# A retention layer with routed experts: where the rows of x are transposed, and by which engine they are copied

## The chip, the cores and the metric

One core of one Trainium2 chip runs the whole program as a single launch. The metric is the device time of that launch in microseconds, the median of several runs. The engines are named as in the profile: PE (TensorE's matmuls) and PEld (its weight loads), DVE (VectorE), ACT (ScalarE), POOL (GpSimd), SP (SyncE, which here only issues transfers).

## The reference

Eight batches of eight heads, 576 positions, 64 values per head. The first part is attention without softmax: scores are multiplied by a decay that falls with distance, and what lies in the future is zero. Its output, one row of 512 values for each of 4,608 tokens, goes through a layer of eight experts, of which each token takes the one with the largest logit.

```python
scores = scale * np.matmul(q, k.transpose(0, 1, 3, 2))
gamma = 1.0 - 2.0 ** (-5.0 - np.arange(H, dtype=np.float32))
rel = pos[:, None] - pos[None, :]
Dmat = np.where(rel >= 0, gamma[:, None, None] ** rel[None, :, :], 0.0)
ret = scores * Dmat[None, :, :, :]
x = np.matmul(ret, v)                      # then (B, S, H, D) -> (B * S, H * D)
...
logits = x @ w_gate
expert_idx = np.argmax(logits, axis=1)
probs = np.exp(logits - logits.max(-1, keepdims=True))
probs /= probs.sum(-1, keepdims=True) + 1e-09
gate_w = probs[np.arange(N), expert_idx]
for e in range(E):
    mask = expert_idx == e
    h = np.maximum(x[mask] @ w1[e], 0.0)
    out[mask] = gate_w[mask, None] * (h @ w2[e])
```

## The kernel before

The order of the work is written out by hand: each engine executes its instructions in the order in which the program issues them, and the framework adds the semaphores. For PSUM the framework orders accesses of different engines by whole banks of a tile.

**The attention stage** is one loop over 40 blocks (L792), five for each batch: c = 0 to 3 are chunks of 128 positions, c = 4 is the remainder of 64. The decay is put into q and k beforehand (scale_q, scale_k, on GpSimd), so that a chunk needs the product of its own scores, masked to the causal half, with v, and the product of its q with a running state. One turn i of the loop works on several blocks at once, in this order on TensorE:

- stage_T transposes k of block i + 2 and, but for c = 0, a quarter of the next batch's q, eight transposes each, into the tile pst2 (L325, L327). ScalarE copies kT (L316) and qT (L302) out.
- stage_R transposes block i - 2 of the finished xT (features by tokens) back into rows of tokens: eight f32 transposes of 64 by 64, in c = 4 four, into the upper 64 of each 128 columns of the score tile pssc, which the scores overwrite later (L459). ScalarE copies one half of the columns and VectorE the other, both to bf16 in the tile xr (L462), and SP writes the rows to x_rows in HBM (L467, L470).
- steps (L812) lets some of the small VectorE instructions of the routing go.
- stage_S adds block i + 1 to the running state in pss (L345), and stage_se copies the state to SBUF on ScalarE (L356). The tile se has two buffers.
- stage_AV multiplies the masked scores of block i with v into psx (L404).
- product (in c = 2 and 3) is a routing product; in c = 0 and 1 stage_L1 and stage_L2 compute the gate's logits of the batch before. All use the PSUM tile of stage_T.
- stage_SC computes the scores of block i + 1 into pssc, two banks, one for each of the two heads of a pair (L374, L387); VectorE multiplies them with the mask into sc (L377, one instruction for each bank) or, for the remainder, with tri (L389, one for both).
- stage_IN adds q times the state to psx (L417; in c = 4 both products of the remainder, L433 and L439), and ScalarE copies the result to xT (L421), in c = 4 to xo, to which VectorE adds the other half (xTr, L444).

Loads of q, k, v go by SP's queue, each held back by a mark (the copy or mask of an earlier block); load_k and load_v run six blocks ahead. The experts' weights and the gathers go by GpSimd's queue, some of them within the loop.

**Routing.** route_batch is a generator of some 25 VectorE instructions for each batch, two products on TensorE among them; a step hands back what it costs, and steps lets go so many as the budget of the turn allows.

**The expert stage** follows from L828 on: gathered rows are transposed, multiplied with w1 and w2 in bf16, scaled by the gate, and scattered to the output. The last two stage_R run there, in the PSUM pool psT.

Of the kernel before, what the change touches and what calls it, by code (L numbers as in the profile page):

```python
# [43 lines left out]
def kernel(  # L44
# [22 lines left out]
    def after(ins, dep):  # L67

        if dep is not None:
# [21 lines left out]
    wk3 = p1.enter_context(tc.tile_pool(name="wk3", bufs=3))  # L91
    wk4 = p1.enter_context(tc.tile_pool(name="wk4", bufs=4))
# [9 lines left out]
             "R": lambda n: [pssc[:, o, :].rearrange("p (a u t) -> p a u t", u=2, t=DH)[:, 0:n, 1, :]  # L102
                             for o in range(2)]}
# [84 lines left out]
    nc.gpsimd.tensor_copy(out=identb[:, :], in_=ident[:, :])  # L188
    nc.vector.tensor_scalar(out=tok[:, 0, :], in0=tok[:, 0, :], scalar1=-1.0, scalar2=None, op0=ALU.mult)
# [30 lines left out]
    pssc = ps1.tile([P, 2, 512], F32, name="pssc")  # L220
# [47 lines left out]
    mark = {}  # L268
# [81 lines left out]
    def stage_se():  # L350

        if not todo_s:
            return
        b, c = blocks[todo_s.pop()]
        se = wkp.tile([P, NP, DH], F32, tag="se")
        mark["se"] = nc.scalar.copy(out=se[:, :, :].rearrange("p a d -> p (a d)"), in_=pss[:, 0:NP * DH])  # L356
        sts[(b, c + 1)] = se
# [3 lines left out]
    def stage_SC(i):  # L361
# [6 lines left out]
        if c < NCH:  # L368
            qT = qTs[b]
            for p in range(NP):  # L370
                for u in range(2):
                    for j in range(2):
                        r = slice(j * DH, (j + 1) * DH)
                        mm(pssc[u * DH:(u + 1) * DH, j, p * P + u * DH:(p + 1) * P], kT[r, p, u * DH:(u + 1) * DH],  # L374
                           qT[r, p, c * P + u * DH:(c + 1) * P], True, True)
            for j in range(2):
                mark["sc"] = nc.vector.tensor_tensor(  # L377
                    out=sc[:, j, :, :], in0=pssc[:, j, :].rearrange("p (a i) -> p a i", i=P),
                    in1=mask[:, :].unsqueeze(1).to_broadcast([P, NP, P]), op=ALU.mult)
        else:  # L380
            qTs[(b, "r")] = kT
            for p2 in range(2):
                for hf in range(2):
                    p = 2 * hf + p2
                    for j in range(2):
                        r = slice(j * DH, (j + 1) * DH)
                        mm(pssc[hf * DH:(hf + 1) * DH, j, p2 * P + DH:(p2 + 1) * P], kT[r, p, DH:P], kT[r, p, 0:DH],  # L387
                           True, True)
            mark["sc"] = nc.vector.tensor_tensor(  # L389
                out=sc[:, :, 0:2, 0:DH],  # L390
                in0=pssc[:, :, :].rearrange("p j (a u i) -> p j a u i", u=2, i=DH)[:, :, 0:2, 1, :],
                in1=tri[:, :].unsqueeze(1).unsqueeze(1).to_broadcast([P, 2, 2, DH]), op=ALU.mult)
# [54 lines left out]
    def stage_R(i):  # L447

        b, c = blocks[i]
# [3 lines left out]
        src = xTs[b][:, c, :] if full else xTs[(b, "r")][:, :]  # L453


        for k in range(n):
            for o in range(2):
                r = slice(o * DH, (o + 1) * DH)
                tr(ps[o][:, k ^ 2 * o if full else k, :], src[r, k * P:(k + 1) * P], ident[r, r])  # L459
        xr = wk4.tile([P, n * P], BF16, tag="xr", name="xr")  # L460
        t0 = b * S + c * P
        for o, copy in enumerate((nc.scalar.copy, nc.vector.tensor_copy)):  # L462
            hs = (slice(0, 4, 3), slice(1, 3))[o]
# [557 lines left out]
```

## Time and profile before

| | |
|---|---|
| median of 3 runs | 372.52 us (371.15 to 372.71) |
| the profiled execution | 369.17 us, its span 367.5 us |
| mean granted TensorE clock | 0.962 of full speed |
| busy in the span: PE, PEld | 321.4 us (87%), 236.4 us (64%) |
| DVE, ACT, POOL | 148.4 us (40%), 156.6 us (43%), 199.5 us (54%) |

The span goes from the first to the last instruction of one profiled execution, which is 1.7 us shorter than that execution's own time. Matmuls are pipelined and their ends are modelled, so a busy PE is not at its peak; the starts of weight loads (PEld) tell best when TensorE got to a piece of work. The attention stage ends at about 202 us.

### The profile page before, as it was taken

What the parts mean: (1) busy time and instruction counts of PE and PEld (TensorE: products, weight loads), DVE (VectorE), ACT (ScalarE), POOL (GpSimd) and SP (SyncE); (2) the same over time, 40 slices, a digit from 0 to 9 for tenths busy, and PEclk for the clock granted to TensorE, in tenths of its full rate; (3) what the DMA queues carried; (4) which work ended last, traced back from release to release, by engine and by line L of the source; (5) the groups of instructions that cost most, each with busy time, mean ns of one, the idle gap of its engine ahead of it and who ended that gap; (6) DMA issues with size and microseconds to landing.
All of it is one profiled execution on the core that took longest, in us unless ns stands there. A gap on an engine that the chain in (4) does not pass through costs nothing. (4 is left out here: it accounts for less than half of the span.)

```text
span 367.5 us, 12120 instructions
## 1 busy us (share of the span) xinstructions
PE 321.4 (87%) x5108; PEld 236.4 (64%) x5108; DVE 148.4 (40%) x442; ACT 156.6 (43%) x331; POOL 199.5 (54%) x255
## 2 busy tenths in 40 slices
PE   5898988979888889787876997999999999999991
PEld 5687867767677677676765765555565656565650
DVE  5234446465564565654735363221121212121211
ACT  3345344352443434444313433345545454545440
POOL 2467534625355236468730026577778778788422
PEclk9599999999999999999996799899999999999997
DMA  8999978979696978999999013379899999999312
GB/s 209 222 221 213 241 188 206 215 194 208 147 230 163 210 181 187 210 224 218 195 192 167 23 58 96 117 134 190 186 212 208 222 193 206 214 192 214 138 58 75
DMA packets 117577, 65.95 MB, mean 179 GB/s; under 512 B 88334, under 2 KB 109838, under 8 KB 117520
## 3 DMA queue, kind: packets, MB, share of 16 engines
q0 software_dynamic: 18432, 31.80, 41.5%
q1 hardware_dynamic: 98560, 33.34, 39.0%
q8 instruction: 41, 0.67, 0.8%
q14 instruction: 16, 0.13, 0.1%
q10 hardware_dynamic: 528, 0.02, 0.1%
HBM read 67.45 MB, written 15.50 MB: 226 GB/s over the span
## 5 line engine op out<-in xcount | busy, mean ns | idle before, releaser
L283 POOL TENSOR_TENSOR kk<-kt,kg 128x512 f32<-128x512 f32 x39 | 40.8, 1045 | 85.9 <-PE pss L62 50.1
L62 PE MATMUL py<-w2b,ht 128*128 128x512 bf16 x320 | 76.0, 384 | 0.3 <-DVE ys L884 0.3
L739 ACT ACTIVATE ht<-pm 128x384 bf16<-128x384 f32 (+1 forms) x96 | 50.6, 527 | 57.3 <-PE pm L62 56.6
L62 PE MATMUL pm<-xt,w1b 128*128 128x256 bf16 (+1 forms) x512 | 73.2, 301 | 0.0
L884 DVE TENSOR_SCALAR ys<-py,gsl 128x512 f32<-128x512 f32 x40 | 30.0, 751 | 105.2 <-PE py L62 100.0
L885 POOL DMA_INDIRECT out_dram<-ys,tids x40 | 40.8, 1019 | 58.0 <-ACT xt L724 24.1
L62 PEld LDWEIGHTS <-w1b 128*128 128x128 bf16 x512 | 50.1, 99 | 22.0 <-issue 0.2
L377 DVE TENSOR_TENSOR sc<-pssc,mask 128x512 f32<-128x512 f32 x64 | 41.3, 686 | 29.5 <-PE pssc L62 24.2
L62 PEld LDWEIGHTS <-ht 128*128 128x128 bf16 x320 | 30.3, 99 | 31.3 <-issue 1.8
L679 POOL DMA_INDIRECT xg<-x_rows,tidg x40 | 41.1, 1026 | 11.8 <-issue 8.4
L62 PE MATMUL pssc<-qT,kT 64*64 64x64 f32 (+1 forms) x1024 | 35.8, 259 | 4.5 <-DVE xr L464 4.5
L62 PE MATMUL psx<-sc,vt 128*64 128x128 f32 (+1 forms) x640 | 39.6, 269 | 0.1
L356 ACT COPY se<-pss 128x256 f32<-128x256 f32 x32 | 12.2, 380 | 49.8 <-PE psx L62 44.2
L724 ACT COPY xt<-pt 128x512 bf16<-128x512 bf16 x40 | 22.8, 586 | 23.2 <-PE pt L65 23.2
L62 PEld LDWEIGHTS psx<-sc,vt 128*64 128x64 f32 (+1 forms) x640 | 32.1, 140 | 0.8 <-ACT xT L421 0.3
L62 PEld LDWEIGHTS pssc<-qT,kT 64*64 64x64 f32 x1024 | 27.9, 135 | 7.3 <-DVE xr L464 5.4
L421 ACT COPY xT<-psx 128x512 f32<-128x512 f32 x32 | 18.8, 586 | 30.1 <-PE psx L62 19.3
L464 DVE CAST xr<-pssc 128x256 bf16<-128x256 f32 (+1 forms) x38 | 15.2, 400 | 37.2 <-ACT xr L464 37.2
L273 POOL TENSOR_TENSOR qq<-qt,qg 128x512 f32<-128x512 f32 x28 | 29.8, 1064 | 0.1
L316 ACT COPY kT<-pst 128x512 f32<-128x512 f32 x40 | 23.7, 592 | 13.5 <-PE pst L65 12.7
L261 POOL DMA_DIRECT2D w2b<-in_moe_w_dram x32 | 23.5, 755 | 4.5 <-DMA w2b<-in_moe_w_dram 2.2
L62 PE MATMUL pss<-vt,kk 128*64 128x64 f32 x512 | 23.3, 234 | 0.5 <-issue 0.5
(130 smaller groups left out, 366.0 us busy)
## 6 DMA issues: line engine op xcount, KB each, us to landing
kt<-in_k_dram SPq DMA_DIRECT2D x32, 256.0 KB, 4.8
qt<-in_q_dram SPq DMA_DIRECT2D x16, 512.0 KB, 5.8
vt<-in_v_dram SPq DMA_DIRECT2D x32, 256.0 KB, 4.4
w1b<-in_moe_w_dram POOLq DMA_DIRECT2D x32, 256.0 KB, 6.5
w2b<-in_moe_w_dram POOLq DMA_DIRECT2D x32, 256.0 KB, 5.6
x_rows<-xr SPq DMA_DIRECT2D x32, 128.0 KB, 5.0
kt<-in_q_dram SPq DMA_DIRECT2D x8, 128.0 KB, 4.7
kt<-in_k_dram SPq DMA_DIRECT2D x8, 128.0 KB, 5.3
```

Source lines behind the costliest of these rows:

```text
L62: nc.tensor.matmul(out=out, lhsT=lhsT, rhs=rhs, start=start, stop=stop, skip_group_check=True)
L261: after(nc.gpsimd.dma_start(out=wb[e][part // n][:, o:o + m, :], in_=w[e, o * P:(o + m) * P, :].rearrange("(c p) f -> p c f", p=P)), dep)
L273: eng.tensor_tensor(out=qq[:, :, :].rearrange("p s (h d) -> p h s d", d=DH), in0=qts[b][:, h0:h0 + 2, :, :], in1=qg[:, 0:NCH, h0:h0 + 2].r ...
L283: eng.tensor_tensor(out=kk[:, :, :], in0=kts.pop(i)[:, :, :], in1=kg[:, blocks[i][1], :].unsqueeze(2).to_broadcast([P, H, DH]), op=ALU.mult)
L316: mark["kT"] = nc.scalar.copy(out=kT[:, :, :].rearrange("p a (u t) -> p u a t", u=2), in_=ps[:, :, o:o + 256].rearrange("p u (a t) -> p u ...
L377: mark["sc"] = nc.vector.tensor_tensor(out=sc[:, j, :, :], in0=pssc[:, j, :].rearrange("p (a i) -> p a i", i=P), in1=mask[:, :].unsqueeze( ...
L421: mark["xT"] = nc.scalar.copy(out=xTs[b][:, c, :].rearrange("p (w t) -> p w t", w=2), in_=psx[:, :, 0:2 * P])
L679: nc.gpsimd.indirect_dma_start(out=xg[:, :], out_offset=None, in_=x_rows[0:nr, :], in_offset=bass.IndirectOffsetOnAxis(ap=slots[ph][1][:, ...
L724: nc.scalar.copy(out=xts[(e, ph)][:, :, j * P:(j + 1) * P], in_=pt[:, :, :])
L739: nc.scalar.activation(out=ht[:, f0:f0 + per, :], in_=pm[:, :, :], func=AF.Relu)
L884: nc.vector.tensor_scalar(out=ys[:, :], in0=py[:, :], scalar1=gsl[:, e, slots[ph][2] + j:slots[ph][2] + j + 1], scalar2=None, op0=ALU.mult)
L885: scatters.append(nc.gpsimd.indirect_dma_start(out=next(outs)[:, :], out_offset=bass.IndirectOffsetOnAxis(ap=slots[ph][0][:, e, j:j + 1], ...
```

## The change

- stage_S now stands in front of stage_R (in c = 4 behind it), and both in front of steps; get_TQ, the copy of qT, stands in front of both.
- The score tile of two banks becomes two tiles of one bank each. Each mask instruction reads one tile; the remainder's mask becomes two instructions.
- stage_xb, new: ScalarE casts block i - 1 of xT from f32 to a bf16 tile xb in SBUF. stage_R transposes that one turn later: eight bf16 transposes (four in c = 4) with 64 weight columns and 128 moving columns, into the first score tile alone, read as bf16. A second identity with its halves swapped (identx) puts the heads in their right order. One ScalarE copy of all columns writes xr; VectorE's copy is gone.
- se has three buffers instead of two.
- In c = 4 stage_IN stands in front of stage_SC.

```diff
--- before.py
+++ after.py
@@ -89,6 +89,7 @@
     ldv = p1.enter_context(tc.tile_pool(name="ldv", bufs=6))
     wkp = p1.enter_context(tc.tile_pool(name="wk", bufs=2))
     wk3 = p1.enter_context(tc.tile_pool(name="wk3", bufs=3))
+    wkb = p1.enter_context(tc.tile_pool(name="wkb", bufs=3))
     wk4 = p1.enter_context(tc.tile_pool(name="wk4", bufs=4))
     wk1 = p1.enter_context(tc.tile_pool(name="wk1", bufs=1))
     attc = p1.enter_context(tc.tile_pool(name="attc", bufs=1))
@@ -99,8 +100,7 @@
     ps1 = pp.enter_context(tc.tile_pool(name="ps1", bufs=1, space=PSUM))
     pst2 = pp.enter_context(tc.tile_pool(name="pst2", bufs=1, space=PSUM))
     pools = {"S": lambda *a: pst2.tile(*a, tag="t2", name="pss2"),
-             "R": lambda n: [pssc[:, o, :].rearrange("p (a u t) -> p a u t", u=2, t=DH)[:, 0:n, 1, :]
-                             for o in range(2)]}
+             "R": lambda n: pssc[0][:, :].bitcast(BF16).rearrange("p (a u t) -> p a u t", u=2, t=P)[:, 0:n, 1, :]}

     blocks = [(b, c) for b in range(B) for c in range(NCOL)]
@@ -186,6 +186,9 @@
     make_identity(nc, ident[:, :])
     identb = consts.tile([P, P], BF16, name="identb")
     nc.gpsimd.tensor_copy(out=identb[:, :], in_=ident[:, :])
+    identx = consts.tile([P, P], BF16, name="identx")
+    for j in range(2):
+        nc.gpsimd.tensor_copy(out=identx[:, j * DH:(j + 1) * DH], in_=ident[:, (1 - j) * DH:(2 - j) * DH])
     nc.vector.tensor_scalar(out=tok[:, 0, :], in0=tok[:, 0, :], scalar1=-1.0, scalar2=None, op0=ALU.mult)
     lrow = attc.tile([P, 2, H], F32, name="lrow")
     for h in range(H):
@@ -217,7 +220,7 @@

-    pssc = ps1.tile([P, 2, 512], F32, name="pssc")
+    pssc = [ps1.tile([P, 512], F32, name=f"pssc{j}") for j in range(2)]
     psx = ps1.tile([P, 2, 512], F32, name="psx")
     pss = ps1.tile([P, 512], F32, name="pss")

@@ -265,7 +268,17 @@

     qqs, qTs, kks, kTs, scs, sts, xTs, lts = {}, {}, {}, {}, {}, {}, {}, {}
-    mark = {}
+    xbs, mark = {}, {}
+
+    def stage_xb(i):
+
+        if i < 0:
+            return
+        b, c = blocks[i]
+        src = xTs[b][:, c, :] if c < NCH else xTs[(b, "r")][:, :]
+        xbs[i] = wkb.tile([P, src.shape[-1]], BF16, tag="xb", name="xb")
+        nc.scalar.copy(out=xbs[i][:, :], in_=src)
+

     def scale_q(b, p, eng=nc.gpsimd):
         h0 = 2 * p
@@ -352,7 +365,7 @@
         if not todo_s:
             return
         b, c = blocks[todo_s.pop()]
-        se = wkp.tile([P, NP, DH], F32, tag="se")
+        se = wk3.tile([P, NP, DH], F32, tag="se")
         mark["se"] = nc.scalar.copy(out=se[:, :, :].rearrange("p a d -> p (a d)"), in_=pss[:, 0:NP * DH])
         sts[(b, c + 1)] = se

@@ -371,11 +384,11 @@
                 for u in range(2):
                     for j in range(2):
                         r = slice(j * DH, (j + 1) * DH)
-                        mm(pssc[u * DH:(u + 1) * DH, j, p * P + u * DH:(p + 1) * P], kT[r, p, u * DH:(u + 1) * DH],
+                        mm(pssc[j][u * DH:(u + 1) * DH, p * P + u * DH:(p + 1) * P], kT[r, p, u * DH:(u + 1) * DH],
                            qT[r, p, c * P + u * DH:(c + 1) * P], True, True)
             for j in range(2):
                 mark["sc"] = nc.vector.tensor_tensor(
-                    out=sc[:, j, :, :], in0=pssc[:, j, :].rearrange("p (a i) -> p a i", i=P),
+                    out=sc[:, j, :, :], in0=pssc[j][:, :].rearrange("p (a i) -> p a i", i=P),
                     in1=mask[:, :].unsqueeze(1).to_broadcast([P, NP, P]), op=ALU.mult)
         else:
             qTs[(b, "r")] = kT
@@ -384,12 +397,13 @@
                     p = 2 * hf + p2
                     for j in range(2):
                         r = slice(j * DH, (j + 1) * DH)
-                        mm(pssc[hf * DH:(hf + 1) * DH, j, p2 * P + DH:(p2 + 1) * P], kT[r, p, DH:P], kT[r, p, 0:DH],
+                        mm(pssc[j][hf * DH:(hf + 1) * DH, p2 * P + DH:(p2 + 1) * P], kT[r, p, DH:P], kT[r, p, 0:DH],
                            True, True)
-            mark["sc"] = nc.vector.tensor_tensor(
-                out=sc[:, :, 0:2, 0:DH],
-                in0=pssc[:, :, :].rearrange("p j (a u i) -> p j a u i", u=2, i=DH)[:, :, 0:2, 1, :],
-                in1=tri[:, :].unsqueeze(1).unsqueeze(1).to_broadcast([P, 2, 2, DH]), op=ALU.mult)
+            for j in range(2):
+                mark["sc"] = nc.vector.tensor_tensor(
+                    out=sc[:, j, 0:2, 0:DH],
+                    in0=pssc[j][:, :].rearrange("p (a u i) -> p a u i", u=2, i=DH)[:, 0:2, 1, :],
+                    in1=tri[:, :].unsqueeze(1).to_broadcast([P, 2, DH]), op=ALU.mult)

@@ -446,23 +460,25 @@

     def stage_R(i):

+        if i < 0:
+            return
         b, c = blocks[i]
         full = c < NCH
         n = NP if full else NP // 2
         ps = pools["R"](n)
-        src = xTs[b][:, c, :] if full else xTs[(b, "r")][:, :]
+        xb = xbs.pop(i)

         for k in range(n):
-            for o in range(2):
-                r = slice(o * DH, (o + 1) * DH)
-                tr(ps[o][:, k ^ 2 * o if full else k, :], src[r, k * P:(k + 1) * P], ident[r, r])
+            w, a = k // (n // 2), k % (n // 2)
+            o = (ps[:, 2 * a:2 * a + 2, w * DH:(w + 1) * DH] if full
+                 else ps[:, w, :].rearrange("p (h d) -> p h d", d=DH))
+            for u in range(2):
+                r = slice(u * DH, (u + 1) * DH)
+                tr(o[r], xb[:, k * P + u * DH:k * P + (u + 1) * DH], (identb, identx)[w][:, :])
         xr = wk4.tile([P, n * P], BF16, tag="xr", name="xr")
         t0 = b * S + c * P
-        for o, copy in enumerate((nc.scalar.copy, nc.vector.tensor_copy)):
-            hs = (slice(0, 4, 3), slice(1, 3))[o]
-            copy(out=xr[:, :].rearrange("p (a h d) -> p a h d", h=NP, d=DH)[:, :, hs, :],
-                 in_=ps[o].rearrange("p (w a) d -> p a w d", w=2))
+        nc.scalar.copy(out=xr[:, :].rearrange("p (a t) -> p a t", t=P), in_=ps)
         if full:
             nc.sync.dma_start(out=x_rows[t0:t0 + P, 0:DW], in_=xr[:, :].bitcast(F32))
         else:
@@ -754,7 +770,8 @@
         put_TQ(psx, p * 256, 0, p)
         get_TQ(psx, p * 256, 0, p)
     keep_busy(8)
-    nc.vector.memset(pssc[:, :, :], 0.0)
+    for j in range(2):
+        nc.vector.memset(pssc[j][:, :], 0.0)
     ps = pair_banks()
     for p in range(2, NP):
         scale_q(0, p, nc.vector)
@@ -804,14 +821,14 @@
         stage_T(i + 2, b + 1, c - 1 if c > 0 and b + 1 < B else None)
         if c in (1, 3) and b + 2 < B:
             load_q(b + 2, c // 2, mark.get("kT"))
-        if i > 1:
-            stage_R(i - 2)
         if todo_q:
             todo_q.pop()()
+        for stage in ((stage_S, stage_R) if c < NCH else (stage_R, stage_S)):
+            stage(i + 1 if stage is stage_S else i - 2)
+        stage_se()
+        stage_xb(i - 1)
         if i > 7:
             steps(rf, (1.5, 1.7, 1.3, 1.3, 1.0)[c])
-        stage_S(i + 1)
-        stage_se()
         stage_AV(i)
         if i > 7 and c in (2, 3):
             product(rf)
@@ -819,8 +836,8 @@
             stage_L1(b - 1)
         elif c == 1 and b > 0:
             stage_L2(b - 1)
-        stage_SC(i + 1)
-        stage_IN(i)
+        for stage in ((stage_SC, stage_IN) if c < NCH else (stage_IN, stage_SC)):
+            stage(i + 1 if stage is stage_SC else i)
         load_v(i + 6, mark.get("xT"))
         if 0 not in slots and len(placed) == B // 2:
             make_slots(0)
@@ -830,10 +847,11 @@
     psH = pq.enter_context(tc.tile_pool(name="psH", bufs=3, space=PSUM))
     psY = pq.enter_context(tc.tile_pool(name="psY", bufs=2, space=PSUM))
     pools["T"] = lambda *a: psT.tile(*a, tag="pt", name="pt")
-    pools["R"] = lambda n: [psT.tile([P, NP, DH], F32, tag="pt", name="psr")[:, 0:n, :] for _ in range(2)]
+    pools["R"] = lambda n: psT.tile([P, NPT, P], BF16, tag="pt", name="psr")[:, 0:n, :]
     pools["S"] = lambda *a: psY.tile(*a, tag="py", name="pss2")
     pools["H"] = lambda *a: psH.tile(*a, tag="ph", name="pm")
     stage_R(NB - 2)
+    stage_xb(NB - 1)
     for j in range(CA // P):
         trans(0, 0, j)
     stage_L1(B - 1)
```

## Rows read from the trace of the kernel before

**Rows 1.** Stretches: us; PE, PEld, DVE, ACT, POOL busy; PEclk; DMA share; GB/s.

```profile
20.00:50.00 30.00, 27.00 (x714) 23.32 (x712) 12.42 (x25) 13.57 (x31) 21.37 (x45) 1.00 0.96 226
50.00:150.00 100.00, 84.11 (x2155) 71.73 (x2155) 57.45 (x175) 44.20 (x103) 40.83 (x42) 1.00 0.84 193
150.00:200.00 50.00, 40.12 (x1008) 33.98 (x1002) 27.87 (x84) 18.72 (x46) 29.34 (x35) 0.96 1.05 205
```

**Rows 2.** List of waits, TensorE's own: us in total, times, longest.

```profile
PEld pssc L65 <- DVE sc L377: 20.4, 30, 1.2
...
PEld pssc L62 <- DVE xr L464: 5.6, 8, 1.0
...
PE pss L62 <- DVE oh L571: 6.0, 7, 1.0
```

**Rows 3.** List of waits, ScalarE's and VectorE's.

```profile
ACT se L356 <- PE psx L62: 44.2, 16, 4.4
DVE xr L464 <- ACT xr L464: 37.2, 38, 1.6
```

**Rows 4.** Timeline, one block (c = 2): start, us, operation [idle before <-releaser].

```profile
91.59 1.29 DVE L377 TENSOR_TENSOR sc<-pssc,mask 128x512 f32<-128x512 f32 x2 [0.63 <-PE pssc L62]
91.88 0.33 PEld L65 LDWEIGHTS pst<-ident,kk 64*128 64x128 f32 x8 [0.17 <-issue]
...
92.12 0.33 PEld L65 LDWEIGHTS pst<-ident,qq 64*128 64x128 f32 x8
...
92.94 0.32 PEld L65 LDWEIGHTS pssc<-ident,xT 64*128 64x128 f32 x8 [0.48 <-DVE sc L377]
...
92.96 0.60 ACT L316 COPY kT<-pst 128x512 f32<-128x512 f32 x1
...
93.33 0.55 PEld L62 LDWEIGHTS pss<-vt,kk 128*64 128x64 f32 x16
...
93.44 0.39 ACT L464 CAST xr<-pssc 128x256 bf16<-128x256 f32 x1
...
93.79 0.86 PEld L62 LDWEIGHTS psx<-sc,vt 128*64 128x64 f32 x16
...
93.86 0.42 DVE L464 CAST xr<-pssc 128x256 bf16<-128x256 f32 x1 [0.98 <-ACT xr L464]
...
95.20 0.84 PEld L62 LDWEIGHTS pssc<-qT,kT 64*64 64x64 f32 x31
...
96.66 0.33 PEld L65 LDWEIGHTS pst<-ident,kk 64*128 64x128 f32 x8 [0.17 <-issue]
```

**Rows 5.** Timeline, the blocks c = 4 (from 101.19) and c = 0 (from 104.86).

```profile
101.19 0.33 PEld L65 LDWEIGHTS pst<-ident,kk 64*128 64x128 f32 x8 [0.17 <-issue]
...
102.00 0.59 ACT L316 COPY kT<-pst 128x512 f32<-128x512 f32 x1
...
103.37 0.84 PEld L62 LDWEIGHTS pssc<-qT,kT 64*64 64x64 f32 x31 [0.74 <-DVE xr L464]
...
104.86 0.33 PEld L65 LDWEIGHTS pst<-ident,kk 64*128 64x128 f32 x8
...
105.75 0.41 DVE L444 TENSOR_TENSOR xTr<-psx,xo 128x256 f32<-128x256 f32 x1
105.89 0.33 PEld L65 LDWEIGHTS pssc<-ident,xT 64*128 64x128 f32 x8 [0.70 <-DVE sc L377]
```

**Rows 6.** Groups by line and form, a ScalarE copy: busy us, mean ns.

```profile
L724 ACT COPY xt<-pt 128x512 bf16<-128x512 bf16 x40 | 22.8, 586 | 23.2 <-PE pt L65 23.2
```

**Rows 7.** Timeline, expert stage: eight bf16 transposes and what follows them.

```profile
344.99 0.54 PEld L65 LDWEIGHTS <-xg 128*128 128x128 bf16 x8
...
345.49 1.45 PEld L62 LDWEIGHTS <-ht 128*128 128x128 bf16 x8
```

**Rows 8.** The page, part 2: granted TensorE clock in 40 slices of the span.

```profile
PEclk9599999999999999999996799899999999999997
```

## The prediction

> **What bounds the kernel now.** I read the table by stretches first. In the attention stage (20 to 200 us) TensorE runs at full clock and moves data nearly all the time, but it is not full: in 50 to 150 it is busy 84.1 of 100 us, while VectorE has 57, ScalarE 44 and GpSimd 41 [rows 1]. So no single engine fills the stage; TensorE is the busiest and the rest of its time is waiting. After 206 us the expert stage is solid matmul and the change touches nothing there. The question is therefore what TensorE waits for in the attention stage, and the list of waits says it in three lines: the row transposes (stage_R) wait for the masks, 20.4 us in 30 times; the score matmuls (stage_SC) wait for VectorE's half of the row copy, 5.6 us in 8; the first routing product waits for the one-hot tensor, 6.0 us in 7 [rows 2]. Together 32.0 us, all in TensorE's own order of work, where nothing behind them can go ahead.
>
> The timeline of one block (c = 2) shows the first kind. The masks run from 91.59 for 1.29 us. TensorE starts the transposes of k and q at 91.88, is free 0.48 us before 92.94, and only then gets to the row transposes, because these write both score banks and the second mask has just released the second bank. The state products (pss) and the score-times-v products stand behind it, though neither of them needs those banks [rows 4]. The block takes 96.66 - 91.88 = 4.78 us.
>
> **The change part by part.** All times below are counted from the start of stage_T's transposes (zero).
>
> *State products in front of the rows.* T ends at 92.94 - 0.48 - 91.88 = 0.58. The state products (93.33 to 93.79, 0.46 us) now follow directly and end at 1.04. *Two score tiles*: the row transposes now write the first tile alone, so they need only the first mask, which ends about 0.64 us (half of 1.29) after 91.59, at 0.35. So the wait for the masks is gone in c = 1 and 2 with 0.7 us to spare, and in c = 3, where there are no state products, with 0.2. The score-times-v products start with head parity 0, so they too need the first mask first; the second ends at 1.00, before they begin. What is late next is the score matmuls' bank, which the single row copy on ScalarE must give back.
>
> *One copy on ScalarE instead of a copy on each engine.* The copies went one after the other: VectorE's waited for ScalarE's 37.2 us in 38 times [rows 3], and ended 94.28 - 93.44 = 0.84 us after ScalarE's began [rows 4]. The new copy is 128x512 bf16 from PSUM, the shape of the copy of xt, 586 ns [rows 6]. ScalarE starts kT 0.81 after T (102.00 - 101.19) [rows 5], and successive copies start 0.48 apart (92.96, 93.44) [rows 4]; the order is now kT, qT, xr, so xr runs from 1.77 to 2.36. In c = 2 the scores are due at 0.58 + 0.46 + 0.43 (rows, below) + 1.41 (93.79 to 95.20) = 2.88: no wait. In c = 3 they are due at about 2.42: none. In c = 4 there are no score-times-v products; the change puts the remainder's products in front of the scores as cover. They end at about 0.58 + 0.39 + 0.46 + 0.65 = 2.1 (0.65 is 104.86 - 103.37 less the 0.84 of the scores), so some 0.3 us of the present 0.74 [rows 5] stays.
>
> The Trainium skill speaks against this edit: TensorEngine Tiling (Array Packing), PSUM Bottleneck, says to use both ScalarE and VectorE for emptying PSUM. By that rule the halves would run side by side, 0.42 us, and one copy of 0.59 would be 0.17 us later in each of 38 blocks: a result 6.5 us worse than mine if nothing covered it. The trace disagrees: the two took turns [rows 3].
>
> *The cast xb* is one more ScalarE instruction per block, 128x512 from SBUF to bf16. The trace has no such form; the nearest are the 256-element cast, 0.39 us [rows 4], and the 512-element copy, 0.59 [rows 6]. I take 0.59, with a pitch of 0.48. It stands behind xr and the state copy se, ends at about 3.1, and its reader is the next block's transposes. What hides it is ScalarE's idle time: 44 of 100 us busy [rows 1]. Behind it in the queue is the copy xT, which waits for the end of the block (2.88 and the 1.46 us from 95.20 to 96.66, so 4.3) anyway. If that cover were gone, it would cost 0.48 us a block, 18 us in all. *se with three buffers* lets the state copy run at once; now it sits in ScalarE's queue until TensorE has ended the block (44.2 us in 16 times [rows 3]), with xT and kT behind it. That wait is off TensorE's path now; without the edit it would hold up xb.
>
> *Transposes in bf16.* Eight of 128 columns each replace eight f32 ones of 64. Bounds: the f32 ones of k take 0.24 us for eight (91.88 to 92.12), and the row group now 0.39 (92.94 to 93.33) [rows 4]; bf16 transposes of 128 columns on the full array take 345.49 - 344.99 = 0.50 for eight [rows 7]. So between -0.15 and +0.11 per block. The score-times-v passes, the same 128 columns on the same half-width tiles, take 0.86 for 16, 0.43 for eight [rows 4]; I take that: +0.04 in 31 blocks, 1.2 us, with -4.6 and +3.4 as ends.
>
> *Routing right behind the masks.* VectorE now sits 0.98 us idle behind the masks and then copies for 0.42 [rows 4] before routing can begin: 1.40 us, which goes. TensorE asks for the one-hot 0.5 us sooner, as its own wait is gone, so the present wait of some 0.86 (6.0 in 7) is covered; for the scan behind the one-hot, which feeds the next product, I leave 0.2 us a batch, an estimate.
>
> *What is made worse.* In c = 4 the scores now follow the remainder's products, and on VectorE the sum xTr (0.41 us [rows 5]) stands ahead of the masks. It waits for xo on ScalarE, behind xb's end at 3.1; with xo taken as a 256-element copy of 0.39, xTr ends at about 3.8, while the scores end at 2.4 + 0.84 + 0.1 = 3.35. So the masks start some 0.45 us late. The next block (c = 0) has only k's transposes, and its rows wait for the first mask: of the present 0.70 [rows 5] about 0.45 stays. The remainder's mask is now two instructions; nothing waits for the second. The moved stage issues one x_rows DMA (two in the remainder) on SP's queue, past no other issue; load_q and load_k stay ahead of it and load_v behind. GpSimd's two copies for identx and the split memset run before the first block.
>
> **The sum.** Removed 32.0. Left over, in seven batches: 0.45 + 0.3 + 0.2 = 0.95 each, 6.7. Transposes 1.2. Transfers: between 50 and 150 the DMA engines moved 193 GB/s; the stage would be 12% shorter (22 of about 180 us), so they must move about 220, against 226 in 20 to 50 at a share of 0.96 [rows 1]. That just fits; I take 2 us for places where it does not (between 0 and 11, see the second case). 32.0 - 6.7 - 1.2 - 2 = 22.1. The profiled execution took 369.2 us (span 367.5), so 347.1; the median of the runs shown is 3.3 higher, which gives 350.4. I predict 350.5.
>
> **The rivals.** 1, the forecast: 350.5, within 344 to 357 by the bounds of the transposes and one or two us of transfers. Chance 0.69.
>
> 2, transfers become the bound. For: in 150 to 200 the share was already 1.05, and only 205 GB/s came [rows 1]. If 205 is all that this mix gives, the stage shrinks by 1 - 193/205 = 6%, 11 us: 361.5. Against: 226 over 30 us, and loads are issued six blocks ahead. The Trainium skill, DMA: Bandwidth & Descriptors, Specifications, gives about 358 GB/s of HBM for a core; by it this case would have no chance and the sum would be 2 us better. No row here comes near that figure. Chance 0.16.
>
> 3, ScalarE takes the place of VectorE: the scores wait for xr in every block. To eat 22 us over 38 blocks it must come 0.6 us past the time it is due, at about 3.0 to 3.5, which needs each of three copies to take 0.8 instead of 0.48. Then 371 to 374, no change. That the new tiles do not part the banks would come out here too, but the state products alone fill the 0.48. Chance 0.04.
>
> 4, slower: starved loads leave TensorE idle, and the clock falls. At the end of the stage it did: the slices of 9.19 us at 193 and 202 show 0.6 and 0.7 [rows 8], a loss of (0.4 + 0.3) x 9.19 = 6.4 us of clock. It decides from four such falls on: 350.5 + 4 x 6.4 = 376. Against it: all slices between 18 and 193 us show 0.9 or more, waits of up to 1.2 us in them notwithstanding. Chance 0.04.
>
> 5, more: with the waits gone, that fall at the end does not come: 344 or a little under. Chance 0.07.
>
> **Range and chances.** 0.5% of 372.5 is 1.9 us, about what a measurement of this kernel can tell from none. Cases 1, 2 and 5 are faster: 0.92; 3 is the same, 0.04; 4 slower, 0.04. The range takes the first case, most of the fifth and half of the second: 341 to 361.
>
> **What would show it.** Right: no row transposes waiting for sc but in the first block of a batch, the score matmuls waiting for ScalarE only behind a remainder, batches about 3 us shorter (22.1 in seven and a little), VectorE's routing starting within 0.1 us of the second mask, DMA near 220 GB/s in the middle. Wrong: long waits of kk or the state products on kt or vt (case 2), the scores waiting for xr in every block (case 3), slices of clock at 0.5 inside the stage (case 4), bf16 transposes above 0.5 us for eight.

## The result and the profile after

| kernel | median, us | runs from..to | profiled execution (its span) |
|---|---|---|---|
| before | 372.39 (4 runs) | 371.15..372.71 | 369.2 (367.5) |
| changed | 350.82 (4 runs) | 348.96..351.62 | 351.4 (349.7) |

The ratio is 0.9419, 95% interval 0.9374 to 0.9465: 21.6 us faster, at 350.8 us where 350.5 was forecast. The total came out; behind it two terms (transposes, transfers) and the size of the waits did not, and the runs below were made to see why. The two profiled executions differ by less, 17.7 us: the attention stage is 20.1 us shorter (below), and the expert stage behind it was 2.4 us longer (164.7 against 162.3).

The table by stretches of the changed kernel answers to [rows 1]. TensorE is now busy 92.9 of the 100 us in the middle, and the DMA engines move 216 GB/s at a share of 0.94; at 20 to 50 us both are nearly full together.

```profile
20.00:50.00 30.00, 29.20 (x784) 25.25 (x781) 12.15 (x28) 21.02 (x45) 21.43 (x45) 1.00 0.96 227
50.00:150.00 100.00, 92.89 (x2451) 79.70 (x2441) 55.67 (x175) 63.98 (x138) 49.54 (x51) 1.00 0.94 216
```

Its list of waits answers to [rows 2]. The rows' wait for the masks (30 times) is down to one, the wait for the one-hot is gone from the list, and the scores wait for ScalarE's row copy. What has grown are TensorE's stops without a releaser ("issue"), 1.7 us in the same line before, and the wait of GpSimd's scaling of k for its rows, 8.3 us before.

```profile
POOL kk L296 <- DMA kt<-in_k_dram: 43.8, 21, 5.9
...
PE pss L62 <- issue: 4.6, 5, 1.8
PE pssc L62 <- ACT xr L481: 3.7, 9, 1.4
...
PE pssc L65 <- DVE sc L390: 0.4, 1, 0.4
```

The timeline of a block c = 2 and the start of c = 3, against [rows 4], and the scores of the remainder behind them:

```profile
62.48 1.29 DVE L390 TENSOR_TENSOR sc<-pssc,mask 128x512 f32<-128x512 f32 x2 [0.68 <-PE pssc L62]
...
62.72 0.46 PE L65 MATMUL pst<-ident,kk 64*128 64x64 f32 x8
...
63.36 0.69 PE L62 MATMUL pss<-vt,kk 128*64 128x64 f32 x16
...
63.82 0.28 PEld L65 LDWEIGHTS <-xb 128*64 128x64 bf16 x8
...
64.04 0.86 PEld L62 LDWEIGHTS psx<-sc,vt 128*64 128x64 f32 x16
...
64.43 0.60 ACT L481 COPY xr<-pssc 128x512 bf16<-128x512 bf16 x1
...
65.17 0.65 ACT L280 CAST xb<-xT 128x512 bf16<-128x512 f32 x1
...
65.46 0.84 PEld L62 LDWEIGHTS pssc<-qT,kT 64*64 64x64 f32 x31
...
66.92 0.46 PE L65 MATMUL pst<-ident,kk 64*128 64x64 f32 x8
...
72.49 1.09 PE L62 MATMUL pssc<-qT,kT 64*64 64x128 f32 x32 [0.23 <-ACT xr L481]
```

Nothing stands idle between the state products (63.36), the rows (63.82) and the score-times-v products (64.04). The eight bf16 transposes take 64.04 - 63.82 = 0.22 us; the f32 ones took 0.39 [rows 4]. The block takes 4.20 us instead of 4.78.

Batches can be cut at the remainder's mask: 30.92, 50.15, 69.87, 90.62, 112.34, 133.40, 157.17. The first two last 19.2 and 19.7 us, the later ones 20.8, 21.7, 21.1 and 23.8; before they lasted 23.1 to 24.1. The two clean ones (the first two, without a stop) as one stretch:

```profile
30.92:69.87 38.95, 38.23 (x1027) 32.98 (x1023) 19.94 (x58) 27.04 (x58) 22.26 (x34) 1.00 0.95 228
```

the same two of the kernel before, with the same number of records, and the four behind the first, for the experiments:

```profile
31.19:77.60 46.41, 39.22 (x1027) 33.64 (x1023) 23.75 (x67) 20.48 (x48) 21.67 (x34) 1.00 0.83 201
54.25:148.54 94.29, 79.80 (x2060) 68.19 (x2054) 54.44 (x164) 41.15 (x96) 40.83 (x42) 1.00 0.84 195
```

Per batch, the first two before: 23.20 us = 19.61 busy + 3.59 idle. The same two after: 19.48 = 19.12 busy + 0.36 idle. So 3.73 us a batch, 3.24 of them idle time and 0.49 busy time. (The four behind the first, before: 23.57 = 19.95 busy + 3.62 idle. The first batch has less of the routing in it, so like is set against like.) The expert stage's first product came at 205.19 before and at 185.06 after.

### The profile page after: what moved, and what is told of

Read it like the earlier page. It is cut to its first block, busy times and chain, and to the rows that moved or that the text cites. A ratio compares the mean times of both kernels' runs of the same rounds, so it can differ in the third digit from the quotient of the medians.

```text
span 349.7 us, 12077 instructions
## 1 busy us (share of the span) xinstructions
PE 315.9 (90%) x5092; PEld 232.6 (67%) x5108; DVE 133.4 (38%) x411; ACT 183.3 (52%) x371; POOL 200.2 (57%) x257
## 5 line engine op out<-in xcount | busy, mean ns | idle before, releaser
L62 PEld LDWEIGHTS <-w1b 128*128 128x128 bf16 x512 | 49.8, 98 | 21.7
L390 DVE TENSOR_TENSOR sc<-pssc,mask 128x512 f32<-128x512 f32 x64 | 41.2, 685 | 31.4 <-PE pssc L62 25.5
L740 ACT COPY xt<-pt 128x512 bf16<-128x512 bf16 x40 | 22.8, 586 | 21.6 <-PE pt L65 21.3
L62 PEld LDWEIGHTS psx<-sc,vt 128*64 128x64 f32 (+1 forms) x640 | 31.1, 138 | 3.8 <-issue 2.5
L481 ACT COPY xr<-pssc 128x512 bf16<-128x512 bf16 (+1 forms) x38 | 21.2, 558 | 9.8 <-PE pssc L65 5.7
L62 PEld LDWEIGHTS pss<-vt,kk 128*64 128x64 f32 x512 | 18.6, 143 | 3.7 <-issue 2.1
```

What stands on the lines that cost most here:

```text
L62: nc.tensor.matmul(out=out, lhsT=lhsT, rhs=rhs, start=start, stop=stop, skip_group_check=True)
L390: mark["sc"] = nc.vector.tensor_tensor(out=sc[:, j, :, :], in0=pssc[j][:, :].rearrange("p (a i) -> p a i", i=P), in1=mask[:, :].unsqueeze( ...
L481: nc.scalar.copy(out=xr[:, :].rearrange("p (a t) -> p a t", t=P), in_=ps)
L740: nc.scalar.copy(out=xts[(e, ph)][:, :, j * P:(j + 1) * P], in_=pt[:, :, :])
```

## The experiments

Each ratio is to runs of the kernel before on the same chip, whose medians were 366.1 us (experiments 1, 2 and 5), 370.2 (6 to 9) and 367.0 (3, 4, 10 and 11).

**1. The order alone.** The f32 rows, two copies and one tile stay:

```
-        se = wkp.tile([P, NP, DH], F32, tag="se")
+        se = wk3.tile([P, NP, DH], F32, tag="se")
...
-        if i > 1:
-            stage_R(i - 2)
         if todo_q:
             todo_q.pop()()
+        if c < NCH:
+            stage_S(i + 1)
+        if i > 1:
+            stage_R(i - 2)
+        if c == NCH:
+            stage_S(i + 1)
+        stage_se()
         if i > 7:
             steps(rf, (1.5, 1.7, 1.3, 1.3, 1.0)[c])
-        stage_S(i + 1)
-        stage_se()
...
-        stage_SC(i + 1)
-        stage_IN(i)
+        for stage in ((stage_SC, stage_IN) if c < NCH else (stage_IN, stage_SC)):
+            stage(i + 1 if stage is stage_SC else i)
```

> The kernel before with the order of work of the changed kernel alone (state products in front of the rows, remainder's products in front of the scores, routing behind the state copy, three buffers for se); the rows stay in f32, copied half by ScalarE and half by VectorE, and the score banks stay one tile. By the working of the prediction: the state products cover the wait of the rows for the second mask in c = 1 and 2 (16 blocks, some 0.48 us each and a little more), about 0.4 us of it stays in c = 3 and 0.7 in c = 0, most of the 0.74 us of c = 4 goes, and the wait for the one-hot stays: about 12 us faster than before, 358 to 363 us. The rival (transfers and instruction blocks come late once the stage moves over some 210 GB/s) gives almost the same here, since the stage would move some 205 GB/s; by it the two parts run alone add up to clearly more (by 4 us or over) than the 21.5 us of the whole, by the first theory to the whole within 2 us.

Measured: 0.9999 (0.9967 to 1.0032), no change; both theories missed. The timeline of a block c = 3 shows one place where the gain went:

```profile
72.89 0.46 PE L65 MATMUL pssc<-ident,xT 64*128 64x64 f32 x8 [0.35 <-DVE sc L377]
...
73.12 0.59 ACT L302 COPY qT<-pst 128x512 f32<-128x512 f32 x1
...
73.60 0.39 ACT L464 CAST xr<-pssc 128x256 bf16<-128x256 f32 x1
...
74.02 0.42 DVE L464 CAST xr<-pssc 128x256 bf16<-128x256 f32 x1 [1.19 <-ACT xr L464]
...
75.02 0.27 DVE L571 TENSOR_TENSOR oh<-scr,m 128x40 bf16<-128x40 f32 x1
...
75.43 0.18 PE L62 MATMUL pss<-oh,su 128*128 128x40 bf16 x1 [1.06 <-DVE oh L571]
```

ScalarE now copies qT ahead of its half, VectorE's half waits for that, and the routing stands behind VectorE's half: TensorE waits 1.06 us for the one-hot, where it waited 0.84 before. In the list of waits the rows' wait on the matmul side fell from 16.1 to 6.4 us, and the one-hot's grew from 6.0 to 7.1:

```profile
PE pss L62 <- DVE oh L571: 7.1, 7, 1.1
PE pssc L65 <- DVE sc L377: 6.4, 15, 1.0
```

So c = 3 grew by 0.2 us; c = 0, where the masks now start later and the rows still wait for both, grew by 0.3, while c = 1 and 2 fell by 0.6 and 0.3. The one-hot is not the whole loss. Two batches at full clock, before and in this run, with the same number of records:

```profile
100.89:148.54 47.65, 40.14 (x1036) 34.22 (x1031) 27.51 (x84) 20.57 (x48) 21.00 (x22) 1.00 0.86 195
```

```profile
100.40:146.48 46.08, 41.06 (x1036) 34.55 (x1031) 27.12 (x85) 20.53 (x48) 20.99 (x22) 1.00 0.87 200
```

Idle time fell by 1.2 us a batch, busy time grew by 0.5, and 0.8 came through. The sixth batch then took 26.3 us (23.6 before). Part of the loss was the clock: 0.98 from 53 to 146 us instead of 1.00. What took the rest is not shown.

**2. The rows alone** (bf16 rows, late cast, one copy; old order, one tile, two buffers of se):

> The changed kernel with the old order of work, one tile for both score banks and two buffers for se: only the rows in bf16, the cast by ScalarE, one copy, and with it VectorE free behind the masks. By the working of the prediction, with the transposes as the trace of the changed kernel shows them (0.2 us for eight instead of 0.39): transposes 6 us, the wait for the one-hot some 5, the wait of the scores for the row copy some 2; the wait of the rows for both masks (20 us) stays. About 12 us faster than before, 357 to 364. If the cast or the single copy came into TensorE's way because se sits in ScalarE's queue ahead of them with only two buffers, the gain would be under 6 us and the row transposes would wait for xb. The rival (late transfers) says that this and the other part add up to 4 us or more over the whole's 21.5.

Measured: 0.9781 (0.9738 to 0.9823), 8 us. Four batches:

```profile
53.02:142.85 89.83, 76.39 (x2056) 67.17 (x2052) 46.95 (x148) 53.62 (x116) 40.84 (x42) 1.00 0.89 205
```

22.46 us a batch: 19.10 busy and 3.36 idle, against 19.95 and 3.62. The transposes are there in full (0.85 a batch, 6.5 us in 7.6 batches), but nearly no idle time has gone. The one-hot is off the list of waits, but now the transposes wait for xb, as ScalarE still stands behind se:

```profile
ACT se L370 <- PE psx L62: 36.2, 16, 3.6
...
PEld L65 <- ACT xb L281: 8.3, 14, 1.3
```

That was the alternative expected with a gain under 6 us. Whether it is the order or the third buffer of se that cures it is not parted: no run has the third buffer alone. The two parts alone make 2.2%, the whole 5.8%: the opposite of what the rival asked for, and not the first theory's sum either. The parts need each other.

**3. The order, and both copies on ScalarE.** Experiment 1 with one word changed:

```
-        for o, copy in enumerate((nc.scalar.copy, nc.vector.tensor_copy)):
+        for o, copy in enumerate((nc.scalar.copy, nc.scalar.copy)):
```

> The order of work of the changed kernel with f32 rows, as in the first experiment, and one edit more: both halves of the row copy on ScalarE, so that VectorE is free for the routing behind the second mask. If the order alone gave nothing because the routing on VectorE stood behind its half of the copy, which stood behind ScalarE's kT, qT and own half (the row's wait then only becomes a wait for the one-hot), that wait goes in six or seven batches (7 us), the blocks c = 3 and c = 0 come down by 0.5 to 1 us each, and the kernel is 8 to 13 us faster than before (ratio 0.965 to 0.978). If the order's gain was lost to something else (the clock, transfers, f32 transposes), the ratio stays at 0.99 to 1.00.

Measured: 0.9627 (0.9575 to 0.9679), a little more than the first theory's range. Between this run and experiment 1 lies only the engine of one 0.42 us copy, and 3.7%, some 13.6 us. In c = 3 the one-hot is ready before TensorE asks for it:

```profile
71.71 0.46 PE L65 MATMUL pssc<-ident,xT 64*128 64x64 f32 x8 [0.42 <-DVE sc L377]
...
72.23 0.27 DVE L571 TENSOR_TENSOR oh<-scr,m 128x40 bf16<-128x40 f32 x1
...
72.34 0.67 ACT L464 CAST xr<-pssc 128x256 bf16<-128x256 f32 x2
...
73.13 0.19 PE L62 MATMUL pss<-oh,su 128*128 128x40 bf16 x1
```

The block takes 3.55 us instead of 4.76 (experiment 1 at full clock). Four batches:

```profile
52.40:138.54 86.14, 80.70 (x2056) 68.46 (x2052) 47.04 (x145) 46.34 (x116) 40.89 (x42) 1.00 0.93 213
```

The batch is 21.54 us, idle 1.36. The profile of experiment 1 also lost more to the clock: 0.97 from 20 us to the end of its stage, 1.00 here.

**4. The changed kernel with half the copy back on VectorE,** each half into a tile of its own:

```
-        nc.scalar.copy(out=xr[:, :].rearrange("p (a t) -> p a t", t=P), in_=ps)
         if full:
-            nc.sync.dma_start(out=x_rows[t0:t0 + P, 0:DW], in_=xr[:, :].bitcast(F32))
+            xv = wk4.tile([P, 2 * P], BF16, tag="xv", name="xv")
+            for o, (copy, dst) in enumerate(((nc.scalar.copy, xr[:, 0:2 * P]), (nc.vector.tensor_copy, xv[:, :]))):
+                copy(out=dst.rearrange("p (a t) -> p a t", t=P), in_=ps[:, 2 * o:2 * o + 2, :])
+                nc.sync.dma_start(out=x_rows[t0:t0 + P, o * P:(o + 1) * P], in_=dst.bitcast(F32))
```

> The changed kernel with the row copy of a full block in two halves again, ScalarE's into one tile and VectorE's into another, each with its own write of rows. If the copies of before took turns because the chip lets one engine at a time read those banks, VectorE's half still starts when ScalarE's has ended and xr is complete 0.8 us after ScalarE's start. If they took turns only because both wrote one tile, they now run side by side, 0.4 us. For the time: the copy's end is not what TensorE waits for outside the remainder, and VectorE's half delays the routing by 0.4 us, so 0 to 4 us slower than the changed kernel (ratio 0.942 to 0.953); by the rule that both engines should empty PSUM it would be up to 3 us faster (0.935).

Measured: 0.9672 (0.9617 to 0.9727), 9 us slower than the changed kernel's 0.9423 (below): outside what I expected. In c = 3:

```profile
71.33 0.39 ACT L484 COPY xr<-pssc 128x256 bf16<-128x256 bf16 x1
...
71.75 0.29 DVE L484 COPY xv<-pssc 128x256 bf16<-128x256 bf16 x1 [1.15 <-ACT xr L484]
...
72.62 0.27 DVE L590 TENSOR_TENSOR oh<-scr,m 128x40 bf16<-128x40 f32 x1
...
73.03 0.18 PE L62 MATMUL pss<-oh,su 128*128 128x40 bf16 x1 [1.49 <-DVE oh L590]
```

The wait for the one-hot is back, 9.5 us in seven times, about as much as the loss:

```profile
PE pss L62 <- DVE oh L590: 9.5, 7, 1.5
```

I had counted VectorE's own half (0.4 us; it took 0.29) and not that it must first sit out ScalarE's kT, qT and xr. The edit also writes the rows of a full block in two transfers instead of one; what that costs is not parted from it. The halves still took turns, with separate tiles; the wait is one for a semaphore, and both halves still lie in one PSUM tile, so whether the chip could run them side by side stays open. The rule weighed in the prediction (the Trainium skill, TensorEngine Tiling (Array Packing), PSUM Bottleneck: empty PSUM with both engines) is not borne out here, because the second engine has later work to do that TensorE waits for.

**5. One score tile.** The changed kernel with the two banks again in one tile:

```
-    pssc = [ps1.tile([P, 512], F32, name=f"pssc{j}") for j in range(2)]
+    psc2 = ps1.tile([P, 2, 512], F32, name="psc2")
+    pssc = [psc2[:, j, :] for j in range(2)]
```

> The changed kernel with the two score banks as one tile again; all else as changed. If the wait of the rows follows the tile: in c = 3 (no state products in front) and in c = 0 the rows wait for the second mask again, 0.4 us and 0.65 us in some 15 blocks, 5 to 8 us slower than the changed kernel, 356 to 359. If it follows the bank that is written: the same as the changed kernel, 351. If late transfers are what sets the time of the stage, the added wait is given back in part: 352 to 355.

Measured: 0.9529 (0.9488 to 0.957), against 0.9423 for the changed kernel: 1.1%, 3.9 us. The wait is back. The rows write the first bank alone and still wait for the second mask, so in this program the wait follows the tile and not the bank:

```profile
PE psc L65 <- DVE sc L391: 8.7, 20, 1.1
```

8.7 us of wait cost 3.9, as in the third of the expected cases. Its three batches from 51.5 to 113.7 us take 20.7 to 20.8 us each, where the changed kernel's go from 19.7 over 20.8 to 21.7, which fits late transfers; no run isolates that.

**6. The changed kernel again,** beside the next runs:

> The changed kernel itself, beside the same runs of the kernel before as the next three, so that the one-tile run and these can be set against it. Ratio to before between 0.937 and 0.947 as first measured, 350 us or, on a chip where before takes 366, some 345. If the score tiles do part the wait of the rows, it is 5 to 8 us under the one-tile kernel's ratio of 0.953 (0.933 to 0.940); if not, 0.95.

Measured: 0.9423 (0.9383 to 0.9463), 350.1 us; the stage ends at 185.7.

**7. No expert weights during the stage:** all 16 parts are fetched behind it.

```
-    early = {i: 1 for i in range(12, NB - 8, 4)} | {i: 1 for i in range(NB - 11, NB)}
+    early = {}
...
     pp.close()
+    fetch(16)
```

> The changed kernel with no expert weights loaded during the attention stage (all 16 parts are fetched when the stage has ended, so the expert stage starts late and the total says little): the DMA engines have some 25 GB/s less to move while the attention stage runs. If late transfers and late instruction blocks stretch the batches in its second half (20.9, 21.9, 20.7 and more instead of 19.4 us), all batches now take 19.3 to 19.7 us, GpSimd's scaling of k waits for its rows under 15 us instead of 44, the stops of TensorE in the middle of a group of matmuls (0.4 to 1.9 us each, eight of them) go, and the stage ends 7 to 12 us sooner (at 173 to 178). If the batches lengthen because of TensorE's own order of work or of its clock, they stay at 20 to 22 us and the stage ends at 182 to 185.

Measured: 0.9365 (0.9324 to 0.9407). The stage ends at 178.25, 7.5 us sooner than in experiment 6, at the near end of the forecast. Five batches:

```profile
30.55:129.65 99.10, 96.22 (x2563) 82.84 (x2559) 55.23 (x171) 67.68 (x145) 48.84 (x60) 1.00 0.91 218
```

19.82 us each, idle 0.58: the later ones (20.5, 19.8 and 19.9 us) are nearly as short as the first two (19.3 and 19.7). The sixth was not (24.0 us, from 129.65; 23.8 in the changed kernel's first run), in the stretch where the gathers of expert rows start; what it waits for there stays open. GpSimd still waits 31.4 us for k, more than I expected, but without TensorE noticing. The edit also takes the issuing of these loads from GpSimd; experiment 9, with more traffic from SP's queue, has no such second effect.

**8. The same edit on the kernel before.**

> The same edit on the kernel before. By the theory of late transfers its transfers already fit (193 GB/s), so its batches stay at 23.1 to 23.5 us and the attention stage ends at most 3 us sooner than at 205; the gain of the change inside the stage, with this traffic away from both, is then 25 us or more instead of 20. By the rival both kernels gain alike.

Measured: 0.9985 (0.995 to 1.002). Five batches of 23.05 to 23.58 us, then one of 28.5 where the gathers start; the stage ended at 208.66, 3.5 us later and not sooner. The change's gain in the stage, without this traffic, is 208.66 - 178.25 = 30.4 us instead of 20.1, but some 8 us of that are the clock, which was 0.87 here from 147.7 us on and 1.00 all through the stage of experiment 7. The first five batches, all at full clock, compare better; the kernel before, the changed one, and this run:

```profile
31.19:148.54 117.35, 99.16 (x2563) 84.81 (x2558) 64.72 (x190) 51.34 (x120) 52.49 (x66) 1.00 0.84 197
```

```profile
30.92:133.40 102.48, 96.91 (x2563) 83.23 (x2559) 55.20 (x170) 67.80 (x145) 53.17 (x66) 1.00 0.93 219
```

```profile
31.08:147.68 116.60, 98.86 (x2563) 84.61 (x2559) 64.65 (x190) 51.33 (x120) 48.95 (x60) 1.00 0.78 189
```

The change gains 117.35 - 102.48 = 14.9 us in them with this traffic, and 116.60 - 99.10 = 17.5 us without it.

**9 and 10. More loads,** in the changed kernel and in the one before:

```
+        if 10 <= i < 28:
+            xl = ldx.tile([P, H, DH], F32, tag="x", name="xl")
+            nc.sync.dma_start(out=xl[:, :, :], in_=k[b, :, 0:P, :].rearrange("h p d -> p h d"))
```

> The changed kernel with 18 more loads of 256 KB (rows of k that nothing reads) on SP's queue, one in each of the blocks 10 to 27. If the transfers are at their limit of some 220 GB/s in this stage, 4.7 MB more take 21 us and most of that shows: 12 to 22 us over the changed kernel. If they still hide behind TensorE, 0 to 3 us.

> The kernel before with the same 18 loads of 256 KB. It moved 193 GB/s between 50 and 150 us where some 220 fit: 2.7 of the 4.7 MB find room in those 100 us, the other 2 MB take 9 us. So 5 to 12 us slower than before, less than half of the 24 us that the same loads cost the changed kernel. If the two lose alike (20 us and more), the changed kernel is no nearer to the limit than the one before, and late transfers do not explain its longer batches.

Measured: 1.0124 (1.0077 to 1.017) for the changed kernel, 7.0% or 26 us over 0.9423; 1.0234 (1.0178 to 1.029) for the one before, 8.6 us. The changed kernel lost three times as much, 4 us above its range. Its batches went from 19.7 to 25.1, 26.4 and 27.6 us, and TensorE now waits for k's scaling, which waits for its rows:

```profile
POOL kk L297 <- DMA kt<-in_k_dram: 74.9, 20, 6.7
...
PEld pst L65 <- POOL kk L297: 14.5, 12, 3.3
```

Some 8 of the 26 us are the clock: it was 0.95 from 20 to 210 us, so (1 - 0.95) x 190 = 9.5 us, against 1.7 in the changed kernel (below). The kernel before kept batches of 23.3 to 23.8 up to 148 us with these loads, and lost only behind that:

```profile
50.00:150.00 100.00, 83.96 (x2147) 71.48 (x2145) 57.35 (x175) 43.87 (x103) 39.25 (x40) 1.00 0.96 216
```

The new loads stand in SP's queue beside those of k; waiting for one's turn there is not parted from the rate of the DMA engines.

**11. Half of the early weights,** as in experiment 7 but with

```
+    early = {i: 1 for i in range(NB - 16, NB, 2)}
...
+    fetch(8)
```

> The changed kernel with 8 of the 16 weight parts loaded during the attention stage (one in every second block from 24 on), the other 8 right behind it. By the theory of late transfers the stage ends some 4 us sooner than the changed kernel's 185.7, and the expert stage has what it needs when it starts, without the stop at 200 to 210 us that the run without early weights shows: 343 to 347 us where before takes 370 (ratio 0.927 to 0.938), faster than the changed kernel. If the weights' place does not matter, 0.942.

Measured: 0.9436 (0.9383 to 0.949): the stage ends at 182.5, 3.2 us sooner where some 4 were expected, but the total missed its range (0.927 to 0.938) and can't be told from the changed kernel's. No version beats it beyond doubt; the run without early weights (0.9365) is the nearest, and its interval overlaps.

## Why the prediction was right, and where it was not

*The order, two tiles, one copy: right, place by place.* In c = 2 the rows follow the state products without a wait, in c = 3 the transposes of k and q; the row copy starts 64.43 - 62.72 = 1.71 us after the block's first transpose and takes 0.60 (forecast 1.77 and 0.59); the scores start at 2.74 and do not wait; in a remainder they wait 0.36 us on the weight-load side, 0.23 on the matmul side (forecast 0.3). The cast takes 0.65, and one wait for it, of 0.4 us, is in the list. In c = 0 the sum kept 0.45 us of wait for the first mask; it left out that the state products stand in front of the rows there too, and the list has one such wait, of 0.4 us. Experiment 5 shows that the split of the tile was needed: it gives 1.1%.

*Transposes: the term was mis-sized, with the wrong sign.* Forecast +0.04 us a block, bounds -0.15 and +0.11; measured -0.17 to -0.2. Experiment 2 has the saving nearly by itself, 0.85 us of busy time a batch; of the changed kernel's busy time 0.49 went, as the new order adds some (0.5 in experiment 1). I priced bf16 transposes by f32 products of as many columns; in bf16 they cost about half of that (0.22 us for eight, where I took 0.43).

*The waits removed: mis-sized.* I added the idle times of weight loads [rows 2]. The matmul side of the same list has shorter ones, as a weight load runs ahead of its matmul:

```profile
PE pssc L65 <- DVE sc L377: 16.1, 30, 1.0
...
PE pssc L62 <- DVE xr L464: 4.5, 7, 0.8
```

With 6.0 for the one-hot that is 26.6, not 32.0. On the other side less was left over: 0.36 us idle a batch in all, where 0.95 was kept back. Net of that, 3.24 us a batch went where (32.0 - 6.7) / 7 = 3.61 was forecast.

*Transfers: 2 us was too little.* Busy and idle together, a clean batch gained 3.73 us where 3.44 was forecast, 26.1 us in seven where 24.1 was. But six batches took 140.94 us before (31.19 to 172.13) and 126.25 after (30.92 to 157.17): 14.7 us gained, where six clean ones make 22.4. Of the 7.7 us given back, 3.8 lie in the first five batches. Experiment 7 brings 3.4 of these back with the weights' traffic away, and more traffic costs the changed kernel more than the one before (9 and 10): late transfers, the second rival, in part. The other 3.9 lie in the sixth batch, which experiment 7 does not shorten; their cause stays open. The most that any of these runs moved is 216 GB/s from 50 to 150 us (at a DMA share of 0.94 to 0.96) and 235 from 20 to 50.

*The total: luck in part.* The stage's 20.1 us are 0.3 ahead of these six batches, 14.7 in them and 5.2 behind; the clean gain came out above its forecast and what was given back far above its 2 us. The sum gave 22.1 us from one profiled execution to another; these two differ by 17.7, and the medians by 21.6. That the forecast lies 0.3 us from the median says less than the single terms do.

*What the sum did not say.* The three waits were added as if each could be taken alone. In c = 3 they stand one behind the other: masks, row copy, routing, one-hot. Experiments 1 and 3 show it: with VectorE's half of the copy in the chain the new order gave nothing in total, and the one-hot's wait grew; with that half on ScalarE nearly two thirds of the change's gain are there, with f32 rows. Experiment 4 shows it from the other side. The sum gave "routing right behind the masks" the one-hot's 6.0 us; 3.7% of the time, some 13.6 us, hung on it.

*The clock at the end:* the fall of [rows 8] came earlier and was shorter. From 178 to 186 us, the end of the stage, the granted clock is 1.00; before, it was 0.51 from 196 to 206, a loss of 0.49 x 10 = 4.9 us. But it fell from 155 to 165, where TensorE's longest wait for the row copy lies (1.4 us):

```profile
155.00:165.00 10.00, 8.14 (x195) 6.93 (x197) 4.31 (x18) 5.99 (x13) 8.08 (x10) 0.83 1.16 238
```

That is a loss of 0.17 x 10 = 1.7 us, so some 3 of the 20.1 us are clock: the fifth case, in part. The clock of the fourth case showed most in experiment 9, with its added loads (0.95). ScalarE as the new bound, and a kernel slower than before, did not come.

## What to carry to other kernels

Before waits are added up, follow each one's releaser to the next wait: where they form one chain, removing one alone can give nothing (experiment 1), and a small edit further down can decide how much of it comes through (experiment 3). Take idle time from the engine that does the work, not from the one that runs ahead of it. Where a stage becomes shorter, divide its bytes by the new time: within a few per cent of the highest rate that the trace has shown, part of the gain can go to late transfers. Set like against like: the same batches, with the same number of records, at the same clock.

## What the runs showed of the hardware that was not expected

TensorE stopped in the middle of a group of like matmuls, with no releaser in the profile, two of the stops at the same instructions in separate runs. The changed kernel's first run and experiment 6, weight loads:

```profile
86.07 0.09 PEld L62 LDWEIGHTS <-rh 64*128 64x128 bf16 x1 [1.32 <-issue]
...
122.53 0.25 PEld L62 LDWEIGHTS pss<-vt,kk 128*64 128x64 f32 x5 [0.67 <-issue]
```

```profile
86.51 0.09 PEld L62 LDWEIGHTS <-rh 64*128 64x128 bf16 x1 [1.03 <-issue]
...
120.85 0.25 PEld L62 LDWEIGHTS pss<-vt,kk 128*64 128x64 f32 x5 [0.80 <-issue]
```

Without early weights (experiment 7) there is no stop at either place, though there is one of 0.84 us elsewhere. In the first run the five stops of 0.9 us or more in the attention stage come after 3734, 4494, 6520, 6772 and 7786 records of matmuls and weight loads: the distances are 3, 8, 1 and 4 times some 253. The stop at 122.53 comes after 5506, seven such distances behind the first, and that of experiment 7 after 3480, one ahead of it. The profile has a queue that moves 0.67 MB of instructions in 41 packets, 16 KB each. The Trainium skill, Runtime: NRT & Kernel Launch, Instruction fetch mechanics, says that instructions are fetched by DMA in blocks of 16 KiB, 256 of them, and that the cost of passing from one to the next is mostly hidden. The distance agrees. If these stops are late blocks, 0.7 to 1.9 us were exposed a time, at a DMA share of 0.94 (50 to 150 us) and more. That these stops are late blocks is argued from place, distance and traffic; no run isolated it.
